# A sparse-attention and expert kernel: q's relu on VectorE, K loaded six tokens a partition, a pair's steps at other units, placings by threes

## The chip, the core and the metric

The kernel runs on one core of a Trainium2 chip. A core has engines that run at the same time and wait for each other by semaphores: PE (matrix products and transposes, into PSUM), DVE and ACT (elementwise work, reading PSUM or SBUF), POOL (elementwise work on SBUF, and the issue of indirect and casting DMAs) and SP (which here only issues DMAs). Sixteen DMA engines move the data. The metric is device time in microseconds for one launch: the median over runs of the whole kernel.

## The reference

Inputs are q, k and v of 4 batches, 8 heads, 768 tokens and 64 numbers a token, and the weights of a dense layer and of eight experts. First comes attention over chosen chunks of 32 keys, then a dense layer plus, for each token, one expert:

```python
k_min, k_max = min and max of k over each chunk of 32 tokens
ub = sum(maximum(q * k_min, q * k_max), axis=-1)     # a bound for each query and chunk
ub = where(chunk is not later than the query, ub, -1e9)
top_chunks = argsort(ub)[..., -6:]                   # six chunks a query
scores = q @ k.T / 8, only in those chunks and only causal
attn = softmax(scores);  out = attn @ v
# x: the 3072 tokens, 512 numbers each (8 heads x 64)
y_dense = maximum(x @ w1_dense, 0) @ w2_dense
e = argmax(x @ w_gate);  p = softmax(x @ w_gate)[e]
y = y_dense + p * (maximum(x @ w1[e], 0) @ w2[e])    # 3072 x 512, float32
```

## The kernel before

**Attention by pairs.** Two heads make a pair: 16 pairs, four to a batch. A pair has 11 *units*. A unit multiplies one or a few tiles of 128 keys with the queries that may see them (`scores`, L556): PE writes `sp`, ACT takes the exponential into `ex` (L567), and where the tile lies on the diagonal POOL masks it (L569). One unit later `av` (L573) multiplies `ex` with v, which has a column of ones, and at the end of a head `norm` (L587) divides and writes the token rows `xbig`. The loop at L726 runs over all 176 units in order and issues the scores two units ahead.

**The steps that prepare a pair** hang on units of the pairs before it, by the `if` ladder at L733 to L765:

- `load` (L79): SP loads k, q and v, float32. k and q lie two tokens to a partition, three such groups; v lies one token to a partition.
- `cast_qk` and `cast_v` (L481, L490): POOL casts to float16.
- `prep_k` (L495): PE transposes k, ACT copies it out of PSUM into `kp`, putting the tokens in order (L501), and DVE takes the chunks' maximum and minimum (L505) and multiplies them with a mask (`kb`, L508).
- `prep_kt` (L510): DVE copies `kp` into the two key tiles `kT` (L512, L513).
- `prep_q` (L515): PE transposes q; ACT takes its relu into `qp` (L523); DVE writes -q into `rT` (L524, and half a tile at L525).
- `prep_ub` (L527): PE adds up the bounds; DVE finds the eight largest of each query and head (L541) and marks the chunks below the sixth (L543).
- `prep_s` (L545): PE transposes the marks, and DVE puts them beside -q into `rT` (L551, L552). So one product yields the score and takes out the unwanted chunks.

**Dense layer and routing inside attention.** `batch_fills` (L238) makes small pieces of work for the batch whose attention has ended: six transposes, the gate, the ranks of the tokens in their experts, six *placings* (L360: POOL scatters the token rows to a DRAM `table`, sorted by expert) and 28 pieces of the dense layer (`l1`, `l2`), whose rows `ys` SP stores to the output (L403). They are spread over the units of the next four pairs (L421 to L428). All tiles of such pieces and of the prepare steps share three PSUM buffers. The dense weights `wd` and the expert weights are loaded by casting DMAs of POOL (L191 to L198) at the first unit of pairs 1 to 13.

**Experts.** After the last pair come 28 *blocks* of 128 sorted rows, and up to three more if they are needed (L885 to L920). The first 11 can be filled before the last batch is placed; block 11 and later ones need its six placings. For a block, SP fetches the rows `xg` (L456, 14 buffers) at a row number that it reads into a register (`load_rows`, L448); PE transposes (L815) and multiplies with the expert's first matrix (L824) and its second (L845), at an offset that PE reads into a register (`load_offs`, L440, read at L435); ACT does the relu (L827) and the gate (`yo`, L852, five buffers); and POOL's indirect DMA adds the 128 rows to the output (L853). Blocks from 11 on must follow the dense stores of the last batch. Before the last block, POOL gathers the dense rows of that block (`dr`, L837). SP also stores zeros behind each expert's rows (`empty`, L862). The last batch's own pieces are spread over the first ten blocks (L877 to L880).

**What sets the order.** A scheduling layer puts the instructions of each engine in one order when the kernel is built, from the order of the calls above, the buffers and the `issue_after` marks (an instruction comes behind another in the order, without waiting for its result). An engine then works through its order and waits where data is not there.

Of the kernel before, what the change touches and what calls it, by code (L numbers as in the profile page):

```python
# [17 lines left out]
def kernel(  # L18
# [12 lines left out]
    nc = tc.nc  # L31
# [47 lines left out]
    def load(p, names="kqv"):  # L79
# [3 lines left out]
        for nm, src in (("k", k), ("q", q), ("v", v)):  # L83
# [15 lines left out]
    latest = {}  # L99

# [17 lines left out]
    nc.vector.memset(exf, 30000.0)  # L118
# [119 lines left out]
    def batch_fills(b):  # L238
# [130 lines left out]
        def l1(g, j, hold, half):  # L369
            late = b == B - 2 and len(dense) >= 17  # L370
# [16 lines left out]
        def l2(g, i, hold, half):  # L387
            late = b == B - 2 and len(dense) >= 17
# [85 lines left out]
    with (  # L474
# [6 lines left out]
        def cast_qk(p):  # L481
# [6 lines left out]
            nc.gpsimd.tensor_copy(q16, s["q"].rearrange("p g t d -> p t g d"))  # L488
# [6 lines left out]
        def prep_k(p):  # L495
            s = st[p]
            pk = pprep.tile([128, S], HF, name="pk", tag="pp")
            for t in range(NT):
                nc.tensor.transpose(pk[:, t * 128 : (t + 1) * 128], s["k16"][:, t].rearrange("p g d -> p (g d)"), ident)
            s["kp"] = kp = ahead.tile([128, S], HF, name="kp")  # L500
            nc.scalar.copy(kp.rearrange("d (T p j) -> d T p j", p=128, j=NJ),  # L501
                           pk.rearrange("d (T j p) -> d T p j", p=128, j=NJ))
# [12 lines left out]
        def prep_q(p):  # L515
# [7 lines left out]
            nc.scalar.activation(qp, pq, AF.Relu)  # L523
            nc.vector.tensor_single_scalar(r0, pq, -1.0, ALU.mult)  # L524
            nc.vector.tensor_single_scalar(r1[64:128], pq[64:128], -1.0, ALU.mult)  # L525

        def prep_ub(p):  # L527
# [5 lines left out]
            for t in range(NT):  # L533
                for n, (src, j) in enumerate(((s["qp"], 0), (s["qp"], 1), (rT[p % NB][0], 1))):
# [10 lines left out]
        def prep_s(p):  # L545
# [6 lines left out]
            nc.vector.tensor_copy(r1[0:64], ps[0:64])  # L552
# [115 lines left out]
        cast_v(0)  # L668
        with after(s0["cast"]):
            cast_qk(1)  # L670
# [40 lines left out]
        wq = [(e, w) for w in range(2) for e in range(E)]  # L711
        ahead_n = 2
# [13 lines left out]
        for i, (p, u) in enumerate(seq):  # L726
# [5 lines left out]
            with tc.issue_after(scored[-1][0].ins), tc.issue_after(scored[-2][1].ins):  # L732
                if p == 0:  # L733
                    if u == 3:
                        prep_k(n2)
                    if u == 6:
                        prep_s(n1)
# [6 lines left out]
                elif p < HP:  # L744
                    if u == 1 and n2 is not None:
                        prep_k(n2)
                    if u == 2 and n1 is not None:
                        prep_s(n1)
                    if u == 3 and n2 is not None:
                        prep_q(n2)  # L750
                    if u == 10 and n2 is not None:
                        prep_kt(n2)
                    if u == 10 and n2 is not None:
                        prep_ub(n2)
                else:
                    if u == 2 and n1 is not None:
# [194 lines left out]
```

## Time and profile before

| | us |
|---|---|
| three runs | 248.10, 251.63, 252.63 (median 251.63) |
| the profiled execution | 250.08 |
| its span, first to last instruction | 248.4 |
| PE, DVE, ACT, POOL busy | 207.8, 176.2, 174.4, 161.6 |
| attention of the last batch ends | about 163.6 |
| PE's last product ends | about 238 |
| last scatter is issued | 242.6 |

Busy time counts an instruction from its start to its end, and neighbours can overlap. A row of a timeline reads: start, duration, engine, line, operation, output <- inputs, shapes, and in brackets the engine's idle time ahead of it and what ended that. A row of the grouped view reads: line, engine, operation, shapes, count, then busy us and mean ns, then idle time ahead and what ended it. A row by source line reads: duration in ns as least/median/most, and the first and last start. SPq and PEldq are the queues in which an engine issues DMAs and reads registers; such instructions do not count as busy.

### The profile page before, as it was taken

The page shows a single profiled execution, that of the slowest core. Times are in us where ns is not written, and L with a number is a line of the kernel's source. Part 1 is how long each engine was busy: PE and PEld are TensorE (multiplying, and loading weights), DVE is VectorE, ACT ScalarE, POOL GpSimd, SP SyncE. Part 2 cuts the span into 40 slices and gives each one's busy share as a digit, 9 for nine tenths or more (in the row PEclk, how much of TensorE's full clock was granted, in tenths as well). Part 3 has the DMA queues.
Part 4 walks back from the last instruction along what each step waited for, and adds up shares of the span by engine and source line. Part 5 has one row for each costly group of instructions (what it writes and reads, how often), then busy time and mean ns, then how long its engine had stood idle before and what let it go on. Part 6 is the DMA issues. An engine that isn't in the chain of part 4 may idle for free. (4 is left out here: it accounts for less than half of the span.)

```text
span 248.4 us, 7579 instructions
## 1 busy us (share of the span) xinstructions
PE 207.8 (84%) x2771; PEld 148.7 (60%) x2771; DVE 176.2 (71%) x555; ACT 174.4 (70%) x325; POOL 161.6 (65%) x199
## 2 busy tenths in 40 slices
PE   1688878888998999988999998989999869979930
PEld 0466555666665676756667765667666557757710
DVE  3889999989989789797798998588423135545410
ACT  5589788878787898696899787815656636646620
POOL 6457997586289677268977427603888543888881
PEclk9999999999999999999999999999999999999985
DMA  7999999999999999989999966167599999977785
GB/s 181 252 254 253 208 226 255 253 205 261 226 180 348 192 295 233 203 176 222 304 190 256 222 116 180 62 163 213 123 267 210 162 245 228 195 133 102 123 118 104
DMA packets 75446, 50.54 MB, mean 204 GB/s; under 512 B 29712, under 2 KB 68496, under 8 KB 75408
## 3 DMA queue, kind: packets, MB, share of 16 engines
q1 hardware_dynamic: 60176, 30.72, 48.1%
q0 software_dynamic: 15232, 19.32, 46.5%
q8 instruction: 23, 0.38, 0.6%
q14 instruction: 15, 0.12, 0.2%
HBM read 41.93 MB, written 18.23 MB: 242 GB/s over the span
## 5 line engine op out<-in xcount | busy, mean ns | idle before, releaser
L567 ACT ACTIVATE ex<-sp 128x512 f16<-128x512 f32 (+1 forms) x176 | 91.5, 607 | 10.5 <-PE sp L563 8.1
L563 PE MATMUL sp<-rT,kT 128*128 128x128 f16 (+3 forms) x384 | 63.9, 261 | 3.6 <-ACT ex L567 1.2
L853 POOL DMA_INDIRECT out_dram<-yo,xg x28 | 44.8, 1600 | 26.0 <-DMA xg<-table 13.1
L569 POOL TENSOR_SCALAR_AFFINE_SELECT ex<-ex 128x512 f16<-128x512 f16 x48 | 32.3, 686 | 34.9 <-ACT ex L567 32.2
L582 PE MATMUL op<-v,ex 128*128 128x65 f16 x672 | 45.5, 194 | 7.4 <-POOL ex L569 5.3
L582 PEld LDWEIGHTS <-ex 128*128 128x128 f16 x672 | 35.6, 98 | 22.5 <-POOL ex L569 9.7
L817 DVE COPY exT<-tp 128x512 f16<-128x512 f16 x28 | 11.9, 424 | 33.2 <-PE tp L815 27.4
L563 PEld LDWEIGHTS <-kT 128*128 128x128 f16 x384 | 28.3, 98 | 7.4 <-issue 4.4
L824 PEld LDWEIGHTS <-w 128*128 128x128 f16 x432 | 26.3, 98 | 8.2 <-issue 2.9
L360 POOL DMA_INDIRECT table<-xbig,slot x24 | 24.9, 1038 | 9.4 <-issue 9.1
L824 PE MATMUL hp<-exT,w 128*128 128x128 f16 x432 | 29.2, 219 | 1.8 <-issue 1.8
L852 ACT ACTIVATE yo<-yp,xg 128x512 f32<-128x512 f32 x27 | 18.6, 687 | 15.0 <-PE yp L845 14.6
L845 PE MATMUL yp<-we,ehT 128*128 x112 | 28.9, 379 | 0.3 <-ACT ys L400 0.2
L379 PE MATMUL hp<-xT,wd 128*128 128x384 f16 x128 | 28.6, 325 | 0.6 <-DVE xT L248 0.6
L505 DVE TENSOR_REDUCE ks<-kp 128x24 f16<-128x768 f16 x28 | 25.5, 946 | 3.7 <-ACT kp L501 3.5
L827 ACT ACTIVATE ehT<-hp 128x512 f16<-128x512 f32 x28 | 16.7, 597 | 14.8 <-PE hp L824 11.3
L395 PE MATMUL yp<-wd,hT 128*128 128x512 f16 x96 | 25.9, 379 | 0.3
L384 ACT ACTIVATE hT<-hp 128x384 f16<-128x384 f32 x30 | 15.0, 499 | 9.5 <-PE hp L379 9.0
L471 DVE COPY w<-we 128x2048 f16 x27 | 19.5, 724 | 1.8 <-PE hp L824 1.7
L593 DVE TENSOR_TENSOR xbig<-op,rs 128x384 f16<-128x384 f32 x32 | 17.5, 548 | 0.9 <-DVE rs L591 0.7
L400 ACT COPY ys<-yp 128x512 f32<-128x512 f32 x21 | 12.8, 607 | 6.2 <-PE yp L395 6.2
L493 POOL CAST v<-vf 128x768 f16<-128x768 f32 x16 | 13.4, 840 | 4.2 <-DMA vf<-in_v_dram 3.0
(149 smaller groups left out, 364.1 us busy)
## 6 DMA issues: line engine op xcount, KB each, us to landing
we<-in_moe_w_dram POOLq DMA_DIRECT2D x16, 512.0 KB, 7.7
kf<-in_k_dram SPq DMA_DIRECT2D x32, 192.0 KB
qf<-in_q_dram SPq DMA_DIRECT2D x32, 192.0 KB
vf<-in_v_dram SPq DMA_DIRECT2D x32, 192.0 KB
out_dram<-ys SPq DMA_DIRECT2D x48, 128.0 KB
xg<-table SPq DMA_DIRECT2D x28, 136.0 KB
table<-zt SPq DMA_DIRECT2D x9, 136.0 KB
wd<-in_moe_w_dense_dram POOLq DMA_DIRECT2D x2, 512.0 KB, 8.8
```

What stands on the lines that cost most here:

```text
L360: sc = nc.gpsimd.indirect_dma_start(out=table, out_offset=bass.IndirectOffsetOnAxis(ap=keep["slot"][:, t : t + 1], axis=0), in_=xbig[b % 2 ...
L379: nc.tensor.matmul(hp, wd[:, ko, j * 128 : (j + 1) * 128], xT[:, ko, g * G * 128 : (g + 1) * G * 128], start=(ko == 0), stop=(ko == NK - 1))
L395: nc.tensor.matmul(yp, hold["h"][:, j, i * 128 : (i + 1) * 128], wd[:, NK + j], start=(j == 0), stop=(j == NK - 1))
L471: nc.vector.tensor_copy(w.rearrange("p j f -> p (j f)"), w1f[:, bass.ds(offs1[i], NK * 512)])
L505: nc.vector.tensor_reduce(out=ks[:, i], in_=kp.rearrange("d (c w) -> d c w", w=32), op=op, axis=mybir.AxisListType.X)
L563: last = nc.tensor.matmul(sp[:, o : o + w], kT[p % NB][g][:, kt * 128 : (kt + 1) * 128], rT[p % NB][g][:, a * 128 : z * 128], start=(o == ...
L567: scored.append((last, nc.scalar.activation(ex[:, 0:o], sp[:, 0:o], AF.Exp, scale=-0.125)))
L569: latest["pool"] = nc.gpsimd.affine_select(out=ex, in_=ex, compare_op=ALU.is_ge, fill=0.0, base=0, pattern=[[0, 4], [1, 2], [2, 64]], chan ...
L582: nc.tensor.matmul(s["op", g][:, t * (D + 1) : (t + 1) * (D + 1)], ex[:, o : o + 128], v16[p % NB][:, g, kt, :], start=first, stop=(last_o ...
L824: nc.tensor.matmul(hp[:, j], s["w1"][:, ko, j * 128 : (j + 1) * 128], s["xT"][:, ko], start=(ko == 0), stop=(ko == NK - 1), skip_group_che ...
L845: nc.tensor.matmul(yp, s["hT"][:, j], w2f[:, bass.ds(offs[i] + j * 512, 512)], start=(j == 0), stop=(j == NK - 1))
L853: sc = nc.gpsimd.indirect_dma_start(out=out, out_offset=to, in_=o, in_offset=None, bounds_check=N - 1, oob_is_err=False, compute_op=ALU.by ...
```

## The change

- **K by six tokens.** From pair 2 on, a partition of the loaded k holds six tokens that follow each other; ACT's copy out of PSUM puts them in order with another stride.
- **q.** DVE writes -q of both heads once from PSUM (into `r1`), copies one half of it in SBUF into `r0`, and takes the relu of q from the same tile in SBUF. ACT's relu out of PSUM goes. In pairs 1 to 3 the second half of the marks is copied by ACT.
- **Steps of a pair** stand at other units, the casts of v and of q and k too; the transposes of a finished batch at units 1 to 6 instead of 0, 2, 4, 6, 8, 10, with gate, ranks and placings a little later.
- **Weights.** The 16 expert loads stand at a list of units from 22 to 159, the dense weights at pair 3 instead of 1.
- **Start.** POOL instead of DVE presets `exf`; k and q of pair 1 are cast ahead of v of pair 0.
- **Last batch before the experts.** Two relus of dense rows move from DVE to ACT.
- **Experts.** The last batch's placings stand three at block 2 and three at block 3 instead of one a block from 1 on; the second product of the first two blocks comes ahead of the fills. All 20 row numbers from block 11 on are read at once instead of by fours, the offsets by fours instead of by tens. Fetches of block 11 and later are no longer put behind the last dense store, and start one block sooner.

```diff
+                elif nm == "k" and p > 1:
+                    nc.sync.dma_start(out=f[:, g], in_=src[b, 2 * hp + g].rearrange("(p t) d -> p t d", t=NT))
...
+    nc.gpsimd.memset(exf, 30000.0)
...
-    nc.vector.memset(exf, 30000.0)
...
-            late = b == B - 2 and len(dense) >= 17
+            late = b == B - 2 and len(dense) >= 21
...
-        for n, f in zip((0, 2, 4, 6, 8, 10) + (12,), out_list):
+        for n, f in zip((1, 2, 3, 4, 5, 6) + (13,), out_list):
             at.setdefault(n, []).append(f)
-        at.setdefault(15, []).append(ranks)
+        at.setdefault(16, []).append(ranks)
         for t in range(NT):
-            at.setdefault(18 + 3 * t, []).append(place(t))
+            at.setdefault(20 + 3 * t, []).append(place(t))
...
-        n, c = (min(4, N1 - k), k) if k < N1 else (min(10, NBLK - k), k - N1 + N1R)
+        n, c = (min(4, N1 - k), k) if k < N1 else (min(4, NBLK - k), k - N1 + N1R)
...
-            nc.scalar.copy(kp.rearrange("d (T p j) -> d T p j", p=128, j=NJ),
-                           pk.rearrange("d (T j p) -> d T p j", p=128, j=NJ))
+            nc.scalar.copy(kp.rearrange("d (p t) -> d t p", t=NT), pk.rearrange("d (t p) -> d t p", t=NT))
...
-            nc.scalar.activation(qp, pq, AF.Relu)
-            nc.vector.tensor_single_scalar(r0, pq, -1.0, ALU.mult)
-            nc.vector.tensor_single_scalar(r1[64:128], pq[64:128], -1.0, ALU.mult)
+            nc.vector.tensor_single_scalar(r1, pq, -1.0, ALU.mult)
+            nc.vector.tensor_copy(r0[0:64], r1[0:64])
+            if p == 0:
+                nc.scalar.activation(qp, r1, AF.Relu, scale=-1.0)
+            else:
+                nc.vector.tensor_scalar(qp, r1, -1.0, 0.0, ALU.mult, ALU.max)
...
-            nc.vector.tensor_copy(r1[0:64], ps[0:64])
+            (nc.scalar.copy if p < 4 else nc.vector.tensor_copy)(r1[0:64], ps[0:64])
...
+        when = (22, 46, 47, 56, 67, 76, 93, 99, 113, 122, 127, 136, 137, 138, 155, 159)
...
                 elif p < HP:
                     if u == 1 and n2 is not None:
                         prep_k(n2)
-                    if u == 2 and n1 is not None:
+                    if u == 4 and n1 is not None:
                         prep_s(n1)
-                    if u == 3 and n2 is not None:
+                    if u == 5 and n2 is not None:
+                        prep_kt(n2)
+                    if u == 8 and n2 is not None:
                         prep_q(n2)
-                    if u == 10 and n2 is not None:
-                        prep_kt(n2)
...
                 else:
-                    if u == 2 and n1 is not None:
+                    if u == 3 and n2 is not None:
+                        prep_q(n2)
+                    if u == 4 and n1 is not None:
                         prep_s(n1)
                     if u == 4 and n2 is not None:
                         prep_k(n2)
-                    if u == 5 and n2 is not None:
-                        prep_q(n2)
-                    if u == 7 and n2 is not None:
+                    if u == 8 and n2 is not None:
                         prep_kt(n2)
...
-                if p == 1:
+                if p == 3:
                     load_dense(st[n2]["cast"])
...
-                for _ in range(2 if p >= 10 else 1):
-                    if p > 1 and wq:
-                        load_expert(*wq.pop(0), st[n2]["cast"])
-            if u == 7:
+            if i in when:
+                load_expert(*wq.pop(0), latest["pool"])
+            if u == 6:
...
-        READY = 8
+        READY = 7
...
-        extra = {0: a[:NT] + [a[NT], ranks], **{1 + t: [f] for t, f in enumerate(places)}}
+        extra = {0: a[:NT] + [a[NT], ranks]}
+        for t, f in enumerate(places):
+            extra.setdefault(2 + t // 3, []).append(f)
...
-                load_rows(min(len(rows) + 4, NBLK))
+                load_rows(min(len(rows) + 20, NBLK))
             while got < min(i + AHEAD + 1, NOFT, N1 + 3 * max(i - READY + 1, 0)):
-                if got < N1:
-                    fetch(got)
-                else:
-                    with tc.issue_after(latest["ys"].ins):
-                        fetch(got)
+                fetch(got)
                 got += 1
...
+            if 0 < i < 3:
+                e2(i - 1)
             for f in extra.get(i, ()):
                 f()
-            if i > 0:
+            if i >= 3:
                 e2(i - 1)
```

More of the change, by code (lines that the diff above doesn't have):

```diff
@@ L387, in l2 @@
         def l2(g, i, hold, half):
-            late = b == B - 2 and len(dense) >= 17
+            late = b == B - 2 and len(dense) >= 21
             def f():
@@ L667 @@
             h = nc.scalar.copy(kT[0][1][0:64], exf)
-        cast_v(0)
-        with after(s0["cast"]):
-            cast_qk(1)
+        cast_qk(1)
+        with after(s1["cast"]):
+            cast_v(0)
         load(2, "v")
```

16 lines of the change are left out of this document (8 added, 8 removed).

## The prediction

> **What bounds the kernel now.** I read the busy time by stage first, because the shares on the page (84% PE, 71% DVE, 70% ACT) average over stages with different limits. The stages are cut where the attention of a batch ends; columns: us, then busy us of PE, weight loads, DVE, ACT, POOL (instructions), clock, DMA share, GB/s.
>
> ```profile
> span 248.4 us, 7579 instructions
> 27.10:35.60 8.50, 6.62 (x107) 4.63 (x105) 8.25 (x26) 6.95 (x14) 7.90 (x24) 1.00 1.20 200
> 51.20:90.30 39.10, 35.36 (x520) 25.77 (x521) 34.52 (x113) 32.00 (x65) 26.15 (x35) 1.00 1.07 242
> 90.30:129.70 39.40, 35.89 (x518) 25.59 (x516) 33.46 (x112) 32.72 (x67) 27.44 (x38) 1.00 1.05 225
> 129.70:163.60 33.90, 31.49 (x441) 22.27 (x437) 28.15 (x102) 27.10 (x54) 19.13 (x27) 1.00 0.77 170
> 163.60:210.50 46.90, 43.21 (x480) 30.41 (x481) 21.93 (x62) 25.62 (x44) 24.93 (x18) 1.00 0.89 199
> 210.50:248.40 37.90, 26.05 (x301) 18.81 (x298) 13.27 (x24) 16.80 (x27) 27.96 (x18) 0.89 0.78 133
> ```
>
> Pairs without dense fills (27 to 36 us) belong to DVE: 8.25 of 8.50. From 51 to 164 us PE leads, and idles 3.74 + 3.51 + 2.41 = 9.7 us. From 163.6 PE works on expert blocks and the last dense rows. After 210.5 POOL, which issues the adding scatters, sets the end. Now the timelines around that last handover, PE, ACT, POOL and SP in turn, with two steps of the chain that ended last ("190.06 2.01" and "197.07 3.58").
>
> ```profile
> 197.07 1.06 PE L824 MATMUL hp<-exT,w 128*128 128x128 f16 x16
> 200.70 0.40 PE L815 MATMUL tp<-ident,xg 128*128 128x128 f16 x4 [2.58 <-DMA xg<-table]
> 202.69 0.39 PE L815 MATMUL tp<-ident,xg 128*128 128x128 f16 x4
> 205.96 0.69 ACT L852 ACTIVATE yo<-yp,xg 128x512 f32<-128x512 f32 x1 [0.43 <-PE yp L845]
> 174.17 1.00 POOL L360 DMA_INDIRECT table<-xbig,slot  x1 [0.30 <-DVE rs L339]
> 188.87 1.34 POOL L360 DMA_INDIRECT table<-xbig,slot  x1 [0.30 <-issue]
> 210.50 1.64 POOL L853 DMA_INDIRECT out_dram<-yo,xg  x1 [3.81 <-DMA xg<-table]
> 242.61 1.03 POOL L853 DMA_INDIRECT out_dram<-yo,xg  x1 [0.31 <-issue]
> 190.06 2.01 SPq L435
> 197.07 3.58 DMA xg<-table
> 202.89 3.17 SPq L403 DMA_DIRECT2D out_dram<-ys  x4
> L435 SPq TENSOR_LOAD <-ro x5: 1645/2006/2754, 181.6 to 195.0; - x5
> DMA to landing us min/median/max: 4.3/5.2/6.1
> ```
>
> Two late things stand there. Block 11, the first that may hold a token of the last batch, has its rows only at 200.7: the last placing is issued at 188.87, then SP still reads row numbers (five reads of some 2.0 us, the last from 195.0) and fetches at 197.07. PE loses about 2.6 us. And block 11's scatter starts at 210.50, though its yo ended at 205.96 + 0.69 = 206.65: it must follow the last dense stores, which SP issued at 202.89 to 206.06. (The releaser named, a fetch, had long landed; the stores fit: 206.06 to 210.2 is 4.1 us of landing.) From there seventeen scatters, 1.64 + 0.3 us each, and the gather of dr follow without a gap to 242.61: 32.1 us from first to last start. What comes sooner at 210.50 comes sooner at the end, up to PE's pace: 1.98 to 2.0 us a block (200.70 to 202.69).
>
> **The last stage, part by part.** *One read of 20 rows, after five of the zeroing stores.* The 20-row read has no row of its own; the nearest are the reads of at most four rows (1.65 to 2.75 us), so below 1.65 is unlikely and five times 2.0 is the upper end. I take 3. It lies beside POOL's placings, so it costs nothing unless it outlasts them.
>
> *Placings by threes, yp of the first two blocks ahead of the fills.* The built order of POOL is: scatter 0, scatter 1, all six placings, scatter 2. Scatter 1 has been issued by about 175 (before, a placing stood at 174.17 ahead of it). Six placings at 1.0 + 0.3 us take 7.8, to about 183 instead of 190.2. They land by about 188 (5.2 us, the scatters' median, as bound). Rows of block 11 then arrive at 188 + 3.6 = 191.6, ahead of PE's need at 198: the 2.6 us go. What is moved back: scatters 2 to 10, queued behind the placings, from 183 at some 1.9 us each, done about 200. Waiting for them are the five yo buffers; yo 7 needs scatter 2 landed at 188.5 and is wanted about 194, so nothing stops.
>
> *Fetches no longer behind the dense stores.* This adds a wait on SP. Fetch 17 and later reuse an xg buffer and wait for the landing of the scatter 14 blocks back. In the built order the last six stores lie behind fetches 19 (two stores) and 20 (four); behind them waits scatter 11. Scatter 6 is issued about 183 + 4 x 1.9 = 190.7 and lands at 195.9; then four stores, 3.2 us, and 4.1 us of landing: 203.2. Block 11's yo is due at 206.65 - 2.6 = 204.0. So scatter 11 starts about 204.0 instead of 210.5, with 0.8 us to spare.
>
> *Expert offsets by fours instead of tens, read by PE.*
>
> ```profile
> L435 PEldq TENSOR_LOAD <-eo x1: 2881/2881/2881, 216.3 to 216.3; - x1
> 219.20 1.05 PE L824 MATMUL hp<-exT,w 128*128 128x128 f16 x16 [1.41 <-issue]
> 184.03 1.05 PE L824 MATMUL hp<-exT,w 128*128 128x128 f16 x16 [0.41 <-issue]
> ```
>
> Ten values stopped PE for 1.41 us; a read in front of block 6 for 0.41. After block 11 there will be four reads of four at 0.4 = 1.6 us, instead of 1.41. Then the last yo is ready at 204.0 + 16 x 1.98 + 1.6 = 237.3; POOL alone would reach its last scatter at 204.0 + 32.1 = 236.1. PE is later: 237.3 instead of 242.6, **-5.3 us**. Bounds: -7 (no stall at the reads) and 0 (the stores not sooner). Starting the fetches one block earlier falls into the lead that there is (191.6 against 198): 0.
>
> **Attention, part by part.**
>
> ```profile
> L523 ACT ACTIVATE qp<-pq 128x768 f16<-128x768 f16 x14 | 11.6, 829 | 0.2
> L501 ACT COPY kp<-pk 128x768 f16<-128x768 f16 x14 | 11.3, 807 | 2.9 <-PE pk L499 2.9
> L552 DVE COPY rT<-ps 64x768 f16<-64x768 f16 x15 | 8.2, 548 | 0.3
> L525 DVE TENSOR_SCALAR rT<-pq 64x768 f16<-64x768 f16 x14 | 7.8, 561 | 0.3
> L512 DVE COPY kT<-kp x15: 310/353/737, 16.7 to 147.3; 64x768 f16<-64x768 f16 x15
> L486 POOL CAST k<-kf 128x768 f16<-128x768 f32 x15 | 12.4, 827 | 0.5 <-DMA kf<-in_k_dram 0.5
> 2.24 0.82 POOL L129 TENSOR_SCALAR_AFFINE_SELECT exf<-exf 64x768 f16<-64x768 f16 x1 [0.86 <-DVE hmask L120]
> 39.85 0.82 POOL L493 CAST v<-vf 128x768 f16<-128x768 f32 x1
> PEld L582 <- POOL ex L569: 9.7, 17, 1.9
> POOL ex L569 <- ACT ex L567: 32.2, 20, 5.8
> wd<-in_moe_w_dense_dram POOLq DMA_DIRECT2D x2, 512.0 KB, 8.8
> 55.26 0.81 PE L379 MATMUL hp<-xT,wd 128*128 128x384 f16 x4
> ```
>
> *Relu of q by DVE.* Per pair ACT loses one 0.83. DVE loses the 0.56 read of PSUM (L525) and gains a copy of half and a relu of all of a tile, both out of SBUF. The copy is L512's: 0.31 to 0.74, median 0.35. The relu is between the same 0.31 and 0.74; I take 0.35 too. Net on DVE +0.14. In pairs 1 to 3 ACT also takes L552, so DVE gets 1.11 - 0.70 = 0.41 shorter and ACT no longer (0.83 out, about 0.8 in by L501).
>
> With DVE 97% busy there, three pairs give 1.2 us; I count **-1.0** (bounds 0 and -1.5). In the twelve later pairs ACT sheds 10 us of the 92 it works; what PE waits for most in its queue, POOL's masks (9.7 us over the span), waits in turn for exponentials (32.2), which stand in ACT's queue behind such relus. Of PE's 9.7 us of idle time from 51 us on I take a third, **-3**, with bounds +2 (twelve times DVE's 0.14 on the path) and -6.
>
> *K six tokens a partition.* The casts of k waited 0.5 us in all for loads, so at most that is won directly; kp's write with another stride I hold at L501's 0.81 (0.80 to 0.93 if it behaves as L523). Counted 0.
>
> *Weights.* The dense weights go out behind the cast of v for pair 5 (39.85), about 43, and land 8.8 us later, 52; first wanted at 55.26, now about 54. Cover 2 us, and beyond it the first fills slip one for one. Expert loads are the same sixteen, cost POOL the same, and the last, at unit 5 of pair 14, goes out about 13 us ahead of the first expert block (8.5 us a pair in that stage): 0.
>
> *Start, and steps at other units.* exf's memset on POOL replaces a 0.86 wait and costs at most what the select of this tile does (0.82): 0. Two relus of dense rows go back to ACT: 0, within the bounds above. Transposes spread otherwise fill PE the same: 0, but they are why the bounds are wide.
>
> **Sum.** Profiled execution: 250.08 (span 248.4 and 1.7 around it). 250.08 - 1.0 - 3.0 - 5.3 = **240.8 us**. The median of the three runs is 251.63, so that is 4.3% below it; this kernel's runs, 248.1 to 252.6, can tell some 2% from no change.
>
> **A page against this change.** Here is a row that hurts it.
>
> ```profile
> 76.47 1.39 DVE L508 TENSOR_TENSOR kb<-ks,hmask 128x96 f16<-128x96 f16 x1
> 76.35 0.83 POOL L488 CAST q<-qf 128x768 f16<-128x768 f32 x1
> 77.13 0.67 POOL L569 TENSOR_SCALAR_AFFINE_SELECT ex<-ex 128x512 f16<-128x512 f16 x1
> L508 DVE TENSOR_TENSOR kb<-ks,hmask x14: 194/198/1390, 21.2 to 146.0; 128x96 f16<-128x96 f16 x14
> ```
>
> A DVE operation of 0.198 us took 1.39: it began inside POOL's cast and ended at 77.86, as POOL's mask did (77.80). The Trainium skill, "SBUF — State Buffer", section "Who interferes with whom", says that DVE copies and scalar operations in their fast two-port modes share a port pair with GpSimd, and the second to issue is blocked for the whole instruction. By that rule both operations added per pair are exposed and the one removed, which reads PSUM, was not; the trace agrees where it shows it, here and in the 0.74 of L512.
>
> **Rivals.** *DVE blocked by POOL (slower).* If each added operation takes the 1.39 us above, DVE gains 2 x 1.39 - 0.56 = 2.2 us a pair. Its slack from 51 to 164 us is 112.4 - 96.1 = 16.3, or 1.36 a pair, so it becomes the bound from 0.96 us an operation; at 1.39 the twelve pairs lose 10.3 and pairs 1 to 3 lose 3 x (2.78 - 1.11) = 5.0: 250.1 + 15.3 - 5.3 = 260. Against: L512's median is 0.35. *Attention gains nothing:* PE is bound by its own order, the shared PSUM buffers as before: 250.1 - 5.3 = 244.8. *The stores stay late:* fetches 19 and 20 hold the dense stores until scatters land; if placings and scatters run 6 us behind my count, scatter 11 stays at 210.5: 250.1 - 4 = 246. For it: only 0.8 us to spare. *The change does not do what it says:* the weights are not even (three loads leave at successive units of pair 12), K changes only from pair 2, and both gains fail: 250.
>
> **How the numbers follow.** Forecast 0.55, its own range 234 to 245 (all the good bounds and the start's 0.86 give 234.7, half the sum 245.4); attention nothing 0.14; stores late 0.14; nothing 0.08; DVE blocked 0.09. Faster by over 2% is below 246.6: 0.55 + 0.14 + half of the third (at its edge), 0.76; same 0.07 + 0.08 = 0.15; slower 0.09. The range 234 to 249 leaves out the last two.
>
> **What would show it.** Right: six placings in a row ending near 183; no PE wait before block 11; scatter 11 near 204; no gap in PE over 0.5 at offset reads; DVE copies near 0.35; PE idle under 8 us between 51 us and the end of attention. Wrong: relu or copy of q over 0.9, dense stores landing after 206, fills waiting for wd near 55.

## The result: 8.9% slower, and the profile after

| | before | after |
|---|---|---|
| median | 252.13 us (4 runs, 248.10 to 254.37) | 272.66 us (4 runs, 271.44 to 273.74) |
| ratio, 95% interval | | 1.089 (1.083 to 1.095) |
| profiled execution, span | 250.08, 248.4 us | 272.26, 270.5 us |
| attention ends | 163.6 us | 178.8 us |
| last scatter is issued | 242.61 us | 264.73 us |

Some executions of one kernel run a few per cent longer than its others; the ratios here and below leave those out, the medians do not.

The forecast was 240.8 us with a range of 234 to 249. It was wrong in sign, and none of its rivals reached this time.

First the page of the changed kernel: the head, the busy times, and three groups of its part 5 (line, engine, operation, shapes, count; then busy us, mean ns; then idle time ahead and what ended it). Line numbers are two to four higher than before.

```profile
span 270.5 us, 7592 instructions
PE 213.1 (79%) x2771; PEld 154.7 (57%) x2771; DVE 177.0 (65%) x563; ACT 192.9 (71%) x316; POOL 163.0 (60%) x200
L573 POOL TENSOR_SCALAR_AFFINE_SELECT ex<-ex 128x512 f16<-128x512 f16 x48 | 33.0, 691 | 55.7 <-ACT ex L571 52.4
L503 ACT COPY kp<-pk 128x768 f16<-128x768 f16 x14 | 38.3, 2737 | 1.1 <-PE pk L501 0.9
L506 DVE TENSOR_REDUCE ks<-kp 128x24 f16<-128x768 f16 x28 | 25.5, 943 | 13.5 <-ACT kp L503 12.4
```

The row to stop at is L503. ACT's copy of k out of PSUM, 807 ns before, takes 2737 ns; it has the same shape, type, tiles and count. Fourteen times the difference is (2737 - 807) x 14 = 27.0 us of ACT. ACT lost fourteen relus of 0.83 us by this change and is still 18.5 us busier than before (192.9 against 174.4). What waits behind it shows in the other rows: POOL's masks wait 52.4 us for exponentials (32.2 before), and DVE's chunk maxima 12.4 us for `kp`.

The same by stage (us; then busy us of PE, weight loads, DVE, ACT, POOL; clock; DMA share; GB/s), and by source line, with the list of those who waited for that line:

```profile
51.20:90.30 39.10, 32.06 (x473) 23.35 (x472) 33.46 (x115) 32.10 (x54) 24.03 (x32) 1.00 0.96 218
90.30:129.70 39.40, 32.40 (x493) 24.21 (x492) 33.24 (x104) 35.32 (x58) 24.37 (x32) 1.00 0.91 204
129.70:178.80 49.10, 40.99 (x578) 29.16 (x574) 37.93 (x137) 41.74 (x74) 30.53 (x39) 1.00 0.83 171
...
L503 ACT COPY kp<-pk x14: 2715/2732/2769, 17.5 to 155.3; 128x768 f16<-128x768 f16 x14
...
  DVE ks L506: 12.4, 10
  PE tp L249: 5.4, 3
  PE hp L381: 1.9, 1
```

Between 51 and 130 us PE led before, with 35.4 and 35.9 us busy; now it has 32.1 and 32.4, and ACT has 35.3 in the second stretch. A copy of 2.7 us holds one of the three PSUM buffers that all preparing steps and dense fills share, and exponentials queue behind it on ACT: PE waits for the copy itself (5.4 and 1.9 us) and, elsewhere, for exponentials. The attention ends 15.2 us later. The remaining 6.9 of the 22.1 us come after it:

```profile
181.05 0.40 PE L819 MATMUL tp<-ident,xg 128*128 128x128 f16 x4 [3.18 <-DMA xg<-table]
...
207.97 1.86 PE L849 MATMUL yp<-we,ehT 128*128 x4 [3.83 <-ACT yo L856]
207.23 0.69 ACT L856 ACTIVATE yo<-yp,xg 128x512 f32<-128x512 f32 x1 [6.14 <-remote]
```

PE waits 3.18 us for the rows of the first expert block, and later 3.83 us for a `yo` of ACT, which itself stands idle for 6.14 us; the two waits make 7.0 us. The kernel before has waits of its own in this part (2.58 us at 200.70), so this shows where time was lost and is no full account.

### The profile page after: what moved, and what is told of

It is laid out like the page before. It is cut to its first block, busy times and chain, and to the rows that moved or that the text cites. A ratio compares the mean times of both kernels' runs of the same rounds, so it can differ in the third digit from the quotient of the medians.

```text
span 270.5 us, 7592 instructions
## 1 busy us (share of the span) xinstructions
PE 213.1 (79%) x2771; PEld 154.7 (57%) x2771; DVE 177.0 (65%) x563; ACT 192.9 (71%) x316; POOL 163.0 (60%) x200
## 4 chain that ended last, share of the span: by engine, by line
PE 25%; POOL 22%; issue 15%; DMA 12%; DVE 10%; ACT 10%; POOLq 1%; SPq 1%; ACTq 0%; DVEq 0%
POOL out_dram L857 11%; PE sp L567 7%; ACT ex L571 6%; DMA out_dram<-yo,xg 5%; POOL table L362 4%; PE hp L381 3%; POOL ex L573 3%; PE op L586 3%; DMA qf<-in_q_dram 3%; ACT kp L503 2%; PE yp L397 2%; DMA out_dram<-ys 2%; PE ub L539 2%; PE tp L249 2%; DMA table<-xbig,slot 1%
## 5 line engine op out<-in xcount | busy, mean ns | idle before, releaser
L571 ACT ACTIVATE ex<-sp 128x512 f16<-128x512 f32 (+1 forms) x176 | 93.6, 609 | 13.9 <-PE sp L567 12.8
L567 PE MATMUL sp<-rT,kT 128*128 128x128 f16 (+3 forms) x384 | 66.2, 265 | 16.2 <-ACT ex L571 14.3
L573 POOL TENSOR_SCALAR_AFFINE_SELECT ex<-ex 128x512 f16<-128x512 f16 x48 | 33.0, 691 | 55.7 <-ACT ex L571 52.4
L586 PEld LDWEIGHTS <-ex 128*128 128x128 f16 x672 | 39.7, 100 | 24.7 <-POOL ex L573 5.3
L586 PE MATMUL op<-v,ex 128*128 128x65 f16 x672 | 49.6, 196 | 2.5 <-POOL ex L573 2.1
L503 ACT COPY kp<-pk 128x768 f16<-128x768 f16 x14 | 38.3, 2737 | 1.1 <-PE pk L501 0.9
L506 DVE TENSOR_REDUCE ks<-kp 128x24 f16<-128x768 f16 x28 | 25.5, 943 | 13.5 <-ACT kp L503 12.4
L849 PE MATMUL yp<-we,ehT 128*128 x112 | 30.2, 387 | 4.6 <-ACT yo L856 3.8
L828 PEld LDWEIGHTS <-w 128*128 128x128 f16 x432 | 27.8, 101 | 7.9 <-issue 2.4
L828 PE MATMUL hp<-exT,w 128*128 128x128 f16 x432 | 30.9, 224 | 1.0 <-ACT hT L386 0.7
L386 ACT ACTIVATE hT<-hp 128x384 f16<-128x384 f32 x32 | 16.7, 521 | 6.2 <-PE hp L381 6.1
L849 PEld LDWEIGHTS <-ehT 128*128 128x128 f16 x112 | 10.2, 99 | 13.1 <-issue 6.2
```

Source lines behind the costliest of these rows:

```text
L503: nc.scalar.copy(kp.rearrange("d (p t) -> d t p", t=NT), pk.rearrange("d (t p) -> d t p", t=NT))
L506: nc.vector.tensor_reduce(out=ks[:, i], in_=kp.rearrange("d (c w) -> d c w", w=32), op=op, axis=mybir.AxisListType.X)
L567: last = nc.tensor.matmul(sp[:, o : o + w], kT[p % NB][g][:, kt * 128 : (kt + 1) * 128], rT[p % NB][g][:, a * 128 : z * 128], start=(o == ...
L571: scored.append((last, nc.scalar.activation(ex[:, 0:o], sp[:, 0:o], AF.Exp, scale=-0.125)))
L573: latest["pool"] = nc.gpsimd.affine_select(out=ex, in_=ex, compare_op=ALU.is_ge, fill=0.0, base=0, pattern=[[0, 4], [1, 2], [2, 64]], chan ...
L586: nc.tensor.matmul(s["op", g][:, t * (D + 1) : (t + 1) * (D + 1)], ex[:, o : o + 128], v16[p % NB][:, g, kt, :], start=first, stop=(last_o ...
```

## The experiments

**1. The copy of k: undone, alone, and with its loops exchanged.** The first kernel takes the new load and the new copy out of the change, the second adds these two alone to the kernel before. The third keeps the load and changes one line, so that the same elements go to the same places in another order:

```diff
-            nc.scalar.copy(kp.rearrange("d (p t) -> d t p", t=NT), pk.rearrange("d (t p) -> d t p", t=NT))
+            nc.scalar.copy(kp.rearrange("d (p t) -> d p t", t=NT), pk.rearrange("d (t p) -> d p t", t=NT))
```

> The changed kernel with the K part alone undone (k loaded as before, kp's copy with the write step of before). Theory: kp's copy by ScalarE is the cause; it returns from 2.73 to 0.80 us, ScalarE works some 27 us less (from 192.9 to about 166), the attention ends near 162 instead of 178.8, and the time is 246 to 256 us. Rival: the steps moved to other units and the relu of q on VectorE are the cause; the copy is 0.80 us all the same, but the attention ends after 170 and the time stays above 262 us.

> The kernel before with the K part alone added. Theory: kp's copy takes 2.7 us x14, ScalarE works some 27 us more (from 174.4 to about 201), the attention ends 10 to 17 us later than 163.6, and the time is 260 to 272 us. Rival (other parts are the cause): the time stays within 5 us of the kernel before, 247 to 257.

> The changed kernel with the loops of kp's copy exchanged: the same load, the same elements to the same places, but ScalarE writes kp in order and reads pk 256 bytes apart, where the changed kernel reads in order and writes 12 bytes apart. Theory, the write step costs: the copy takes 0.8 to 1.1 us and the time is that of the K part undone, 246 to 256 us. Rival, the load or any step off the order costs, on either side: the copy stays at 2 us or more and the time stays above 262 us.

Measured: without the K part 254.22 us, ratio to before 1.007 (1.000 to 1.014). The K part alone 279.62 us, ratio 1.108 (1.098 to 1.118), 7.6 us above its expected range and 7.0 above the whole change: beside the slow copy the rest of the change saves time, and why was not followed up. With the loops exchanged 254.19 us, ratio 1.001 (0.996 to 1.007). The page's head and the line of the copy in the third:

```profile
span 252.4 us, 7592 instructions
L503 ACT COPY kp<-pk x14: 793/798/847, 17.4 to 140.6; 128x768 f16<-128x768 f16 x14
```

So the whole loss is the order in which one instruction writes. The kernel before ran through `kp` in order and read PSUM 256 bytes apart; the changed one reads PSUM in order and writes 12 bytes apart. The load of six tokens a partition costs nothing, and gains nothing either: with it and without it the times are 254.2 us. What the rest of the change is worth beside a fast copy is then also told: nothing, where 9.3 us were forecast.

**2. What a write step costs.** Copies whose result nothing reads stand ahead of the kernel before, one line for each step, for example:

```diff
+        for _ in range(2):
+            nc.scalar.copy(dst.rearrange('d (p t) -> d t p', t=3), src.rearrange('d (t p) -> d t p', t=3))
```

> The kernel before with copies put ahead of its work that nothing else reads, each twice: 128x768 half-precision elements out of PSUM into SBUF, with a write step of 1, 2, 3, 4, 6, 8 and 12 elements, by ScalarE and by VectorE; then by ScalarE out of SBUF with steps 2 and 6, out of PSUM with a read step of 6 and writes in order, and with step 6 on both sides. Theory A, a threshold: ScalarE takes 0.8 us up to some step and 2.7 us at every step above it. Theory B, in proportion: about 1.3 us at 3 elements, 1.8 at 4, 2.7 at 6, 3.6 at 8, 5.4 at 12. Both expect 2.7 us for step 6 out of SBUF too and 0.8 us where only the reads step. Of VectorE neither says anything: 0.8 us throughout, or like ScalarE.

The groups by line: ACT with steps of 1, 2, 3, 4, 6, 8 and 12 elements (L111 to L123), DVE with 1, 2, 6 and 12 (L125, L127, L133, L137), then ACT out of SBUF with step 6 (L141), with the step of 6 on the read side alone (L143) and on both (L145).

```profile
L111 ACT COPY mdst<-msrc 128x768 f16<-128x768 f16 x2 | 1.6, 796 | 0.0
L113 ACT COPY mdst<-msrc 128x768 f16<-128x768 f16 x2 | 2.0, 1013 | 0.1
L115 ACT COPY mdst<-msrc 128x768 f16<-128x768 f16 x2 | 2.9, 1435 | 0.1
L117 ACT COPY mdst<-msrc 128x768 f16<-128x768 f16 x2 | 3.7, 1855 | 0.1
L119 ACT COPY mdst<-msrc 128x768 f16<-128x768 f16 x2 | 5.4, 2704 | 0.1
L121 ACT COPY mdst<-msrc 128x768 f16<-128x768 f16 x2 | 7.1, 3552 | 0.1
L123 ACT COPY mdst<-msrc 128x768 f16<-128x768 f16 x2 | 7.0, 3518 | 0.1
...
L125 DVE COPY mdst<-msrc 128x768 f16<-128x768 f16 x2 | 1.1, 558 | 28.3 <-ACT mdst L123 28.3
L127 DVE COPY mdst<-msrc 128x768 f16<-128x768 f16 x2 | 2.0, 1008 | 0.1
L133 DVE COPY mdst<-msrc 128x768 f16<-128x768 f16 x2 | 5.4, 2702 | 0.1
L137 DVE COPY mdst<-msrc 128x768 f16<-128x768 f16 x2 | 7.0, 3516 | 0.1
...
L141 ACT COPY mdst<-mssb 128x768 f16<-128x768 f16 x2 | 5.5, 2737 | 0.1
L143 ACT COPY mdst<-msrc 128x768 f16<-128x768 f16 x2 | 1.6, 799 | 0.1
L145 ACT COPY mdst<-msrc 128x768 f16<-128x768 f16 x2 | 5.4, 2704 | 0.1
```

Theory A falls, and B holds up to 8 elements: from 2 on each element of step adds 0.42 us (1.01, 1.44, 1.86, then 2.70 at 6 and 3.55 at 8), and at 12 (24 bytes) the time is that of 8 (16 bytes). From a step of 2 on ACT and DVE have the same prices, and reading PSUM with a step is free (0.80); a read of SBUF with a step was not tried by itself. The changed kernel's 2.73 us is simply the price of step 6.

**3. Where the last stage's 5.3 us went.** The kernel before with the last stage's edits alone (from `READY = 7` to the end of the diff, and the offsets by fours); then the same with each of two corrections:

```diff
+                if got < N1:
+                    fetch(got)
+                else:
+                    with tc.issue_after(latest["ys"].ins):
+                        fetch(got)
-                fetch(got)
```

```diff
-            extra.setdefault(1 + n * 9 // len(d), []).append(f)
+            extra.setdefault(1 + n * 7 // len(d), []).append(f)
```

> The kernel before with the last stage's edits alone (placings by threes, rows read at once, offsets by fours, fetches not behind the dense stores, yp of the first blocks sooner). Theory as in the prediction: the scatter of block 11 starts near 204 instead of 210.5 and the time is 5.3 us less, some 247 us (245 to 249). Rival: the stall near 200 us of the changed kernel (ScalarE and VectorE both idle for 6 us) belongs to the placings in a row; it is seen here too, and the time is 250 to 256 us.

> The kernel before with the last stage's edits (253.43 us), but the fetches from block 11 on again behind the dense stores, as before. Theory: the fetches held the last dense stores (nine fetches took from 192.65 to 203.25 us, the last four stores left from 206.25 to 208.64, and the scatter of block 11 waited for them until 214.75); with the stores ahead, that scatter starts 3 us or more sooner and the time is 249 to 251 us. Rival: TensorE's pace and its stall near 185 us set the end, and the time stays within 1 us of 253.4.

> The kernel before with the last stage's edits, and the last dense rows spread over seven blocks instead of nine, so that their stores are ready about two blocks (4 us) sooner. Theory, as for the run beside it: the scatter of block 11 starts 3 us or more before 214.75, the time is 249 to 251 us. Rival: within 1 us of 253.4.

Measured: the edits alone 253.43 us, ratio 1.001 (0.996 to 1.005), a time that the rival gave. With the fetches behind the dense stores again 247.72 us, ratio 0.977 (0.971 to 0.982); with the dense rows over seven blocks 247.27 us, ratio 0.981 (0.975 to 0.987); both lie below their expected 249 to 251. So the gain was there, about as large as forecast, and either edit to the dense stores brings it back. What happens is read from the kernel of experiment 1 with the loops exchanged, which has this last stage too. Its SP queue, and block 11's `yo` and scatter:

```profile
193.29 10.72 SPq L458 DMA_DIRECT2D xg<-table  x9
204.11 1.12 SPq L405 DMA_DIRECT2D out_dram<-ys  x2
205.47 0.39 SPq L458 DMA_DIRECT2D xg<-table  x1
205.97 2.40 SPq L405 DMA_DIRECT2D out_dram<-ys  x4
211.16 0.69 ACT L856 ACTIVATE yo<-yp,xg 128x512 f32<-128x512 f32 x1 [0.43 <-issue]
213.84 1.64 POOL L857 DMA_INDIRECT out_dram<-yo,xg  x1 [1.95 <-ACT yo L856]
```

Nine fetches take 10.7 us; in two of them SP waits, 3.8 us in all, until a scatter 14 blocks back has freed the buffer. The last four stores come behind them at 205.97, later than before the change (202.89), and the scatter of block 11 has to follow their landing: it starts 2.0 us after its `yo` has ended (211.85). The `yo` in its bracket is block 12's, which ended just then. With the dense rows over seven blocks as the one further edit:

```profile
196.44 3.00 SPq L405 DMA_DIRECT2D out_dram<-ys  x4
206.60 0.69 ACT L856 ACTIVATE yo<-yp,xg 128x512 f32<-128x512 f32 x1 [0.43 <-PE yp L849]
207.64 1.57 POOL L857 DMA_INDIRECT out_dram<-yo,xg  x1 [0.31 <-DMA xg<-table]
```

The scatter starts 6.2 us sooner. Only 1.6 of them are a shorter wait behind its `yo` (0.4 us instead of 2.0); the other 4.6 were lost ahead of it. With the loops exchanged the `yo` of block 3 begins at 190.25, with the seven blocks at 185.62, and in front of the first lies the idle stretch of experiment 6, which the kernel with the seven blocks does not show. The stores can hold the end without that stretch too: in the fifth kernel of experiment 6, which does not show it either, the `yo` of block 11 ended at 206.01, the last store was issued by 206.64, and the scatter started at 212.10.

**4. The relu of q.** With the loops exchanged, the relu goes back to ACT, as before the change (three hunks undone: q's operations, the tile that the bounds read, the copy of the marks):

> The changed kernel with the copy's loops exchanged and the relu of q again on ScalarE (q's three operations as before, the second half of s copied by VectorE throughout). Theory: with the relu on VectorE that engine is 94 to 97% busy from 51 to 130 us and the attention ends no sooner than before (163); with it back on ScalarE VectorE works 4 us less, and the attention ends 0 to 2 us sooner: 252 to 255 us. Rival, as predicted: the relu on VectorE takes 4 us off the attention; with it back on ScalarE the attention ends near 167 and the time is 257 us or more.

Measured 251.75 us, ratio 0.997 (0.989 to 1.004): the predicted rival (257 us) falls. With the stores still late this kernel's end could not show a gain, so three kernels were run with the seven blocks of experiment 3: the relu on ACT, the relu on DVE, and the relu on ACT with both corrections:

> The changed kernel with the copy's loops exchanged, the relu of q on ScalarE (together 251.75 us, attention done at 159.5), and the last dense rows over seven blocks. Theory: what the attention gained (4 us) reaches the end once the stores leave sooner: 247 to 249.5 us. Rival: the wait for the first rows and the half clock behind it give it back: 250.5 to 252.5 us.

> The changed kernel with two corrections: the loops of the copy of k exchanged, and the last dense rows over seven blocks instead of nine; the relu of q stays on VectorE. Theory: the relu on VectorE costs 2 to 4 us of attention against the kernel with the relu on ScalarE (245.21 us, ratio 0.973 to before): 247 to 250 us, ratio 0.98 to 0.99. Rival, as predicted: the relu on VectorE gains 4 us: 242 us or less, ratio under 0.965.

> The kernel with the copy's loops exchanged, the relu of q on ScalarE and the last dense rows over seven blocks (245.21 us), with the fetches from block 11 on again behind the dense stores as well. Theory: the stores no longer set the end there (its scatters follow at 1.98 us, TensorE's pace, from block 11 on), so this adds nothing: 244 to 247 us. Rival: the two add up, 243 us or less.

Measured: relu on ACT 245.21 us, ratio 0.973 (0.968 to 0.979), below its expected range; relu on DVE 248.35 us, ratio 0.988 (0.984 to 0.993); relu on ACT with both corrections 246.09 us, ratio 0.972 (0.961 to 0.984). The interval of the relu on DVE does not meet the first and just touches the third. So the relu on DVE costs some 2 to 4 us (2.3 and 3.1 in the medians, 3.8 by the ratios 0.973 and 0.988) where the forecast had it gain 3 to 4. The two corrections do not add up. The kernel with the relu on ACT and the seven blocks, 245.2 us, is faster than both kernels of this case.

Why the relu costs: first DVE and ACT over 51 to 130 us, with the relu on DVE, then on ACT (columns as above).

```profile
51.20:90.30 39.10, 36.99 (x546) 26.89 (x544) 38.12 (x131) 32.40 (x65) 26.87 (x36) 1.00 1.11 258
90.30:129.70 39.40, 35.42 (x527) 25.75 (x525) 37.74 (x117) 31.82 (x64) 28.29 (x37) 1.00 1.02 227
```

```profile
51.20:90.30 39.10, 36.56 (x538) 26.72 (x536) 34.37 (x115) 33.60 (x68) 25.79 (x34) 1.00 1.08 238
90.30:129.70 39.40, 37.51 (x557) 27.41 (x554) 35.26 (x118) 36.09 (x72) 30.02 (x40) 1.00 1.07 238
```

DVE is 75.9 of 78.5 us busy with the relu and 69.6 without it, and PE does less in the same time (72.4 against 74.1); the attention ends at 162.0 instead of 159.5. The two added operations have these durations (least, median, most), first in the changed kernel, then in the one with the seven blocks and the relu on DVE. Below them stand two relus of the changed kernel, the first with a POOL cast beside it and the second with none:

```profile
L525 DVE COPY rT<-rT x14: 341/576/955, 24.0 to 154.3; 64x768 f16<-64x768 f16 x14
L529 DVE TENSOR_SCALAR qp<-rT x14: 335/418/990, 24.5 to 155.0; 128x768 f16<-128x768 f16 x14
...
L525 DVE COPY rT<-rT x14: 342/680/1032, 23.3 to 139.3; 64x768 f16<-64x768 f16 x14
L529 DVE TENSOR_SCALAR qp<-rT x14: 336/815/990, 23.8 to 140.1; 128x768 f16<-128x768 f16 x14
...
112.60 0.96 DVE L529 TENSOR_SCALAR qp<-rT 128x768 f16<-128x768 f16 x1
112.42 0.94 POOL L488 CAST k<-kf 128x768 f16<-128x768 f32 x1
113.31 0.95 POOL L490 CAST q<-qf 128x768 f16<-128x768 f32 x1
...
70.58 0.34 DVE L529 TENSOR_SCALAR qp<-rT 128x768 f16<-128x768 f16 x1
```

**5. The moved steps alone.** The kernel before with the moved steps, the weights' units and the start, and nothing of k, the relu or the last stage:

> The kernel before with only the moved steps, the weights' units and the start from the change: k and its copy, the relu of q and the whole last stage as before. Theory: the attention ends 3 to 4 us sooner than 163.6, as in the kernel with the relu on ScalarE (159.5), but the end gains at most 2 us of it: 250 to 253 us. Rival: without the new load of k the attention ends at 162 to 164, since that load made the gain, and the time is that of the kernel before or above.

Measured 251.32 us, ratio 0.995 (0.991 to 1.000). Its end gains at most 1%. Whether its attention ends sooner was not settled.

**6. The handover, and the stretch without work.** Two theories of the last stage were tried on the kernel with the loops exchanged: that the six placings in a row cause the idle stretch near 185 us, and that sooner placings in the attention take away PE's wait for the first rows. The first kernel places the last batch one a block, the second has the whole last stage as before; the third has the attention's placings at the units of before, the fourth at `18 + 2 * t`, the fifth and sixth that with the relu on ACT, and with seven blocks.

```diff
-            extra.setdefault(2 + t // 3, []).append(f)
+            extra.setdefault(1 + t, []).append(f)
```

> The changed kernel with the copy's loops exchanged, and the last batch's placings again one a block (from block 1) instead of by threes; the rest of the last stage as changed. Theory: the six placings in a row cause the stretch in which ScalarE and VectorE stand idle for 5 to 6 us near 185 to 190 us though the matmuls they wait for have ended; here no such stretch is left, TensorE loses 3 to 4 us less, and the time is 250 us or less (from 254.2). Rival: the idle stretch comes with the other edits of that stage (the dense stores ahead of the fetches, the zeroing stores, the offset reads) and is still there; the time stays at 253 to 256 us.

> The changed kernel with the copy's loops exchanged and the whole last stage as before (placings one a block, rows by fours, offsets by tens, fetches behind the dense stores). Theory: the last stage's edits gain nothing as a whole, what they win (no wait for block 11's rows) is spent in the idle stretch, so the time is 252 to 255 us, the same as with them. Rival: they cost 3 us or more, and without them the time is below 251 us.

> The changed kernel with the copy's loops exchanged and the third batch's ranks and placings again at the units of before (15, and 18 + 3t instead of 16 and 20 + 3t; the outputs' steps too). Theory: the last placing of that batch then lands about 1.3 us sooner, TensorE's wait of 2.3 us for the first expert block's rows shrinks by as much or goes, and the time falls by 1 to 2 us, to about 252.5 us. Rival: that wait is refilled by the idle stretch behind it, and the time stays within 0.7 us of 254.2.

> The changed kernel with the copy's loops exchanged and the placings in the attention at units 18 + 2t (the relu of q stays on VectorE). Theory: TensorE's wait of 2.3 us for the first rows shrinks by about 1 us, and the stretch at half clock behind it (3.4 us) may go: 251 to 253 us, from 254.2. Rival: no change, 253.5 to 255.

> As the kernel with the relu of q back on ScalarE (251.75 us), with the placings in the attention at units 18 + 2t instead of 20 + 3t, so that the last stands five to seven units sooner. Theory: what the attention gains is given back at the handover, where TensorE waits 2.8 us for the first expert block's rows and then runs 6.8 us at half its clock; with sooner rows the wait shrinks to 1 us or less (the dense stores ahead of the fetch on SyncE's queue allow 1.7 us of it), and if the stretch at half clock goes with it, 3 us more: 247 to 250 us. Rival: the end is set by the scatters, held by the last dense stores, and does not move: 251 to 253 us.

> The same, and the last dense rows spread over seven expert blocks instead of nine, so that their stores leave sooner. Theory: the scatter of block 11, which waits for these stores (8 us between two scatters before it with the relu on ScalarE), starts 3 us or more sooner, and the time is 2 us or more below the kernel without this edit. Rival: TensorE is the limit there, the scatters only move together, and the time is within 1 us of it.

Measured, in this order: 254.46 us (ratio 1.021, 1.010 to 1.031), 253.89 (1.017, 1.010 to 1.024), 258.13 (1.035, 1.029 to 1.042), 259.32 (1.033, 1.026 to 1.040), 252.66 (1.010, 1.006 to 1.013), 250.09 (0.998, 0.993 to 1.002). Of the expected gains only the last came: the seven blocks take 2.6 us off the fifth kernel. One placing a block has no idle stretch, as its theory expected, but is no faster, and most kernels with the placings in a row have none either (below), so the theory on the placings falls. With the whole last stage as before the median is the same, as expected. Sooner placings in the attention make it slower by 4 to 5 us in the medians with the relu on DVE (8 by the ratios; the third kernel has the outputs' steps of before as well), by 1 us with it on ACT (3 by the ratios) and by 4.9 us with the seven blocks (250.09 against 245.21; 6 by the ratios). PE's wait for the first rows did not shrink with the relu on DVE (3.38 and 2.42 us, from 2.27); with the relu on ACT it fell to 0.67 us and, with the seven blocks, from 2.82 to none, and the time got no better. In their profiles the attention ends at 165 to 171 us, where it ended at 161 to 163 in the first two and with the loops exchanged alone. Why they slow it was not settled.

What the idle stretch is, with the loops exchanged:

```profile
185.15 1.02 PE L849 MATMUL yp<-we,ehT 128*128 x4 [1.24 <-issue]
190.25 0.69 ACT L856 ACTIVATE yo<-yp,xg 128x512 f32<-128x512 f32 x1 [5.15 <-remote]
190.60 0.42 DVE L821 COPY exT<-tp 128x512 f16<-128x512 f16 x1 [6.38 <-remote]
```

The product that ACT waits for ended at 186.17, and ACT begins 4.1 us later; DVE resumes with it. It is seen in the changed kernel, with K undone, with the loops exchanged and with the last stage alone, and in no other kernel of this study, though most of those issue the placings in a row too. Its cause stays open. Of the 6.2 us between the two scatters of experiment 3, 4.6 come with it; what taking it away alone would save is not shown, since the stores could then hold the scatter for longer.

After some waits of PE the granted clock is lower for some microseconds. The first row is the kernel with the loops exchanged, where PE had waited 2.27 us for the first rows just ahead; the second is the kernel before, where it had not.

```profile
165.00:170.00 5.00, 4.96 (x56) 4.82 (x57) 3.62 (x9) 0.60 (x1) 0.00 (x0) 0.66 0.63 176
```

```profile
165.00:170.00 5.00, 5.00 (x80) 4.05 (x78) 3.98 (x14) 2.03 (x5) 0.00 (x0) 1.00 0.59 143
```

PE is full in both, and does 56 products where it did 80 (partly of other kinds). So at this place the wait seems to cost more than its length. The length of a wait does not decide it: behind 2.83 us at 190.98 with the loops exchanged the clock was 1.00 from 190 to 195, behind 2.84 us at 191.03 with K undone it was 0.69 in the same 5 us, and behind 2.58 us at 200.70 the kernel before stayed at 1.00.

## Why the prediction was wrong, point by point

- **"K six tokens a partition": the step that failed.** It said "kp's write with another stride I hold at L501's 0.81 (0.80 to 0.93 if it behaves as L523)", counted 0. Measured 2.73 us, 27.0 us of ACT, 18.5 us of time (272.66 against 254.19). L501 was no row for a strided write: its loops run T, p, j over `kp`, which is the order in memory, so it writes in order and reads with a step; L523 writes in order as well. None of the rows quoted held a write with a step. The bounds should have been open above, and with an open bound the chance of "slower" could not have been 0.09.
- **"Relu of q by DVE": wrong sign.** The forecast was -1.0 and -3; the runs show some 2 to 4 us lost. ACT did get lighter (168.4 us busy with the loops exchanged, 174.4 before), but the attention ended at 163.0 against 163.6, so the third of PE's idle time did not come. The step that failed is the 0.35 us for each added operation: the medians were 0.58 and 0.42 in the changed kernel and 0.68 and 0.82 in the one with the seven blocks, with single ones up to 1.03 there. The rival "DVE blocked by POOL" named the mechanism, with 1.39 us an operation and 0.96 as the point of decision; the measured means, 0.62 for the copy and 0.69 for the relu in the kernel with the seven blocks, lie under it, and still DVE was busy there for 96.6% of the time from 51 to 130 us. That 0.96 rests on DVE's slack of 16.3 us from 51 to 164 us; up to 130 us the slack was 78.5 - 68.0 = 10.5. The row of 1.39 was of a product of two tiles (L508), another operation than the two that were added. Of the added operations themselves, the relu of 0.34 against the one of 0.96 beside a cast agrees with the rule that was cited from the Trainium skill, "SBUF — State Buffer", section "Who interferes with whom"; POOL's cast of k began first and the relu was held up.
- **"Fetches no longer behind the dense stores": the 0.8 us to spare were not there.** The forecast of -5.3 for the last stage had the right size: with the stores ahead it is 0.977 of before. As the change has it, it is 1.001. The prediction put the six placings at 175 to 183; with the loops exchanged the first stands at 180.14 and scatter 6 at 199.09 instead of 190.7, so the fetches that wait for scatters held the last stores to 205.97. That is the rival "the stores stay late", given 0.14, and its condition (6 us behind the count) was met. Besides, the prediction had no term for the idle stretch: block 11's own `yo`, counted at 204.0, ended at 211.85, and 4.6 us of that come with the stretch (experiment 3).
- **The first block's rows: a term that was missing.** PE waits 2.27 us (loops exchanged) to 3.18 us (changed) for these rows, where it waited 0.42 before, and with the loops exchanged its clock is 0.66 over the 5 us behind it. The wait is there with K undone (2.37) and with the relu on ACT (2.82), and it is 0.29 with the attention as before, the last stage's edits and the seven blocks; so it comes with the moved steps, the weights' units or the start. That the later ranks and placings make it is not shown: with the placings at the units of before it was 3.38.
- **Right:** no wait of PE for the rows of block 11; the weights, the start and the moved steps, run together, within 1% of nothing (0.995); the offset reads by fours without a gap over 0.5 us.

## What to carry to other kernels

When an access pattern of a copy changes, look at which side is walked in order: here, with 768 half-precision elements a partition, a step on the write side cost 0.42 us for each further element of step from 2 to 8, a step on the read side of PSUM nothing, and exchanging the loops of one line was worth 18.5 us. A trace without a row of that kind gives no upper bound, and the estimate must say so. And an edit that lets a queue run ahead is priced by what then stands behind its waits: here the fetches that could start sooner held the stores that a scatter near the end has to follow.

## What the hardware showed beyond expectation

- The write step's price is linear in bytes from 4 to 16 and no higher at 24 (1.01 us at 4 bytes, 3.55 at 16, 3.52 at 24), and there it is the same for ACT and DVE to within 1%. The Trainium skill, "SBUF — State Buffer", section "Door 1: The DMA port swizzle (why `[64,N]` ≈ `[32,N]`)", says that consecutive accesses within a 16-byte line have full bandwidth, so that one may step 8 bf16 elements for free. For writes the measurement decides against it: 2 elements cost DVE 1.01 us instead of 0.56. For reads no run here shows it, since the one read with a step that was tried by itself (6 elements, 0.80 us) came out of PSUM.
- Behind a wait of 2.27 us PE ran at a clock of 0.66 over 5 us; in the kernel before, which has no such wait, it stayed at 1.00 there. Kernels that differ by one short wait can so differ by more than that wait, but need not: behind other waits of 2.58 and 2.83 us the clock was 1.00.
